# A decode kernel with grouped-query attention: the side's single-engine loads as three 64 KB rows in two source pieces, its multiplication later, its slot kept longer

## The chip, the cores and the metric

The kernel runs on one core of a Trainium2 chip. The metric is the device time in microseconds (us) of one execution. A core has five engines with their own instruction streams (TensorE for matrix products, VectorE, ScalarE, GpSimd and SyncE) and sixteen DMA engines, which carry all transfers from the chip's large memory (HBM) into the on-chip memory of 128 partitions. SyncE issues most transfers here, GpSimd a few.

## The reference

Two layers, each a decode step of attention with a cache and a gated feed-forward block, with the same weights and the same cache in both layers. Two sequences (b), one token each, 32 query heads on 8 key heads, 32768 cached positions of 128 numbers, all in 32 bits:

```python
for _ in range(2):
    h = layernorm(x)                                   # x: (2, 1, 512)
    q = (h @ wq).reshape(2, 1, 32, 128).transpose(0, 2, 1, 3)
    k, v = repeat(k_cache, 4, axis=1), repeat(v_cache, 4, axis=1)
    p = softmax(einsum("bhqd,bhkd->bhqk", q, k) * 128 ** -0.5)
    x = x + merge_heads(einsum("bhqk,bhkd->bhqd", p, v)) @ wo
    h = layernorm(x)
    gate, up = h @ W_gate, h @ W_up
    x = x + (relu(gate) * up) @ W_down
```

The keys and the values are 16 pairs (head, sequence) of 16 MB each; a layer reads all of them.

## The kernel before

**Turns and halves.** One pair of key head and sequence is a turn; a layer has 16. A turn's keys come in two halves of 8 MB (128 rows of 64 KB), its values too. A half has four pages of eight blocks of 512 columns. The on-chip memory has three slots of one half each, and behind them a small ring for everything else. The list `by_use` holds the slots in order of use: a load takes the first, and `used(s)` moves it to the end. A load into a slot waits, on SyncE, until the work that read the slot before is done; the loads behind it in SyncE's stream wait too.

**Order.** The loop `for i in range(1, NG)` takes the keys of turn i (`keys`, lines 427 to 460) and then the values of turn i - 1 (`values`, lines 462 to 495). `keys` is a generator that issues a half's load and then goes through its pages j = 0 to 7: `k_tile` multiplies a page, and at certain pages other work is put in between: the rest of the softmax of the turn before (`soft_tail`), the output of the turn before that (`head_out`), and in every second turn its projection (`project`, with a load of 1 MB of `wo`). All engines go through their instructions in the order in which this code issues them.

**The side.** In turn 11 of each layer (`SIDE_TURN`), the last 6 blocks of page 3 of the values (1.5 MB, a tenth of the turn's values) are not loaded as a part of their half but in another layout, which the host has prepared, and with another share for each DMA engine. `load_side` (line 315) takes a slot for it and issues four loads. One goes on SyncE's queue (line 318): 20 partitions, 48 KB each, in three pieces of 16 KB, a source of 5 rows, so that five DMA engines carry it. Three are single-engine loads on GpSimd's queue (line 322), each 4 partitions from row 28, 64 or 92 on, 48 KB each in three pieces of 16 KB: source and destination have no common factor in their outer sizes (3 and 4), so that one DMA engine carries all of it. Between them `turn_by` (line 307) issues a tiny transfer of single numbers over 7 or 6 DMA engines, which moves GpSimd's choice of the engine for the next load on by as many. The kernel is built with 512 bytes of room for GpSimd's descriptors (`SCRATCH`, line 32).

`side_keys` (line 281), called from `soft_tail` of turn 11, puts the probabilities into the side's layout: transposes on VectorE of windows of p into two tiles t and u, zeros from GpSimd, and two products with masks. `v_side` (line 325) multiplies them, 24 chunks of 512 columns on 96 partitions, into the accumulator of turn 11. It is issued in `keys(13)` at page 1 (line 450), followed by the evacuation of the accumulator on VectorE. At page 2 come `head_out` of turn 11 and the projection, with the load of `wo`.

**Slots around the side.** With a, b for the two other slots and s for the side's, `by_use` is [a, b, s] after `load_side`. The first half of turn 13's keys takes a, the second b; the first half of turn 12's values takes s, the second a.

Of the kernel before, what the change touches and what calls it, by code (L numbers as in the profile page):

```python
# [8 lines left out]
F32 = mybir.dt.float32  # L9
# [5 lines left out]
D = 512  # L15
# [27 lines left out]
SIDE_TURN = NG - 5  # L43
SIDE_PAGE, SIDE = 3, 6
SIDE_WAYS, SIDE_ROWS, SIDE_CHUNKS, SIDE_GAP = 5, 20, 24, 64
SIDE_END, ALONE, TURNED = 96, (28, 64, 92), (7, 0, 6)
SIDE_THIRD = SIDE_CHUNKS * D // 3 + 16

C_SAME, C_MEAN, C_SEL, C_PAIR, C_SIDE, C_ONE, C_MHALF, C_END = 0, 128, 160, 192, 224, 226, 227, 229

# [2 lines left out]
def attention_reglu_decode(ctx: ExitStack, tc: tile.TileContext, x, k, v, wq, wo, wgu, wd, consts, side, alone, out):  # L53
# [12 lines left out]
    def ring(at, width):  # L66
        if at < 0:
            assert at * KB + width <= 0 or (spill[0] + 1) * SLOT == RING
            at += (spill[0] + 1) * SLOT - RING
        at = int((RING + at) * KB)  # L70
        return arena[:, at : at + width]

    def slot(s, at=0, width=SLOT * KB):
        at = int((s * SLOT + at) * KB)
        return arena[:, at : at + width]
# [57 lines left out]
    col = sel[:, :NB]  # L133
    pair = cst[:, C_PAIR : C_PAIR + 32]
    side_rows = cst[:, C_SIDE : C_SIDE + 2]
    turned = sb.tile([4 * max(TURNED), NLAYER * len(TURNED)], F32, name="turned")
    mhalf = cst[:, C_MHALF : C_MHALF + NB]
    oT = sb.tile([P, REP, NB], F32, name="oT")
    qz = sb.tile([P, 2, QZ], F32, name="qz")
# [139 lines left out]


    def side_keys(p):
        W = SIDE_CHUNKS * 32
        t, u = (ring(SIDE_KEYS_AT + e * W / KB, W) for e in range(2))
        at = SIDE_PAGE // 2 % 2 * D + (SIDE_PAGE % 2 * 8 + 8 - SIDE) * 32

        def windows(c, start, step, n):
            rows = p[32 * c : 32 * c + 32]
            return bass.AP(rows.tensor, rows.offset + at + start, [rows.ap[0], [step, n], [1, 32]])

        def chunks(t, c, lo, n):  # L290
            return t[32 * c : 32 * c + 32, 32 * lo : 32 * (lo + n)].rearrange("p (k r) -> p k r", r=32)

        for g, c in enumerate((0, 1, 3)):
            nc.vector.transpose(chunks(t, 0, 8 * g, 8), windows(c, 0, 20, 8))
            nc.vector.transpose(chunks(u, 0, 8 * g, 8), windows(c, 132, 4, 8))
        nc.vector.transpose(chunks(t, 2, 0, 24), windows(2, 0, 4, 24))
        nc.vector.transpose(chunks(u, 2, 0, 24), windows(2, 68, 4, 24))
        for c in (1, 3):
            nc.gpsimd.memset(t[32 * c : 32 * c + 32], 0.0)
            nc.gpsimd.memset(u[32 * c : 32 * c + 32], 0.0)  # L300
        nc.vector.tensor_scalar_mul(t, t, side_rows[:, 0:1])
        nc.vector.scalar_tensor_tensor(t, u, side_rows[:, 1:2], t, ALU.mult, ALU.add)
        return t

    def turn_by(n):
        if n:
            few = consts[: 5 * n, :1].rearrange("(e r) f -> e r f", r=5)[:, :4]
            nc.gpsimd.dma_start(turned[: 4 * n, steps[0] : steps[0] + 1], few)  # L310
        steps[0] += 1

    steps, side_at = [0], {}

    def load_side(L, n):
        s = by_use[0]
        vt = side_at[n] = slot(s, 0, 3 * SIDE_THIRD).rearrange("p (a f) -> p a f", a=3)[:, :, : SIDE_CHUNKS * D // 3]
        load(vt[:SIDE_ROWS], side[L, :, : 4 * SIDE_CHUNKS * D])
        part = 4 * SIDE_CHUNKS * D // 3
        for e, (row, step) in enumerate(zip(ALONE, TURNED)):  # L320
            turn_by(step)
            nc.gpsimd.dma_start(vt[row : row + 4], alone[L, e, :, :part])
        used(s)

    def v_side(n):
        vt, t, J = side_at.pop(n), side_of.pop(n), SIDE_PAGE // 4
        for k in range(SIDE_CHUNKS):
            nc.tensor.matmul(  # L328
                acc[32 * (k % 4) : 32 * (k % 4) + 16, :],
                t[:SIDE_END, 32 * k + 16 * J : 32 * k + 16 * J + 16],  # L330
                vt[:SIDE_END, k // 8, k % 8 * D : (k % 8 + 1) * D],
                start=False, stop=k >= SIDE_CHUNKS - 4,
            )

    def v_tile(n, j, vt, first, last, blocks):
# [87 lines left out]
    for L in range(NLAYER):  # L423
        last = L == NLAYER - 1
        seq = list(range(NG)) if L % 2 == 0 else list(range(NG - 1, -1, -1))

        def keys(i):
            n = seq[i]
            if i < NG - 1:
                place_queries(i + 1, seq[i + 1])  # L430
            if L and i == 0:
                loads = list(kept_k)
                kept_k.clear()
            elif L and i == 1:
                f, g = key_slots
                loads = cuts(k, n, [(f, 0, 0, 8), (f, 16, 8, 16), (f, 32, 16, 32), (g, 0, 32, 48), (g, 32, 48, 64)])
            elif i == NG - 1:
                f, g = key_slots[:] = by_use[:2]
                loads = cuts(k, n, [(f, 0, 0, 32), (g, 0, 32, 48), (g, 32, 48, 64)])
            else:  # L440
                loads = whole(k, n)
            if not last and i == NG - 1:
                loads = list(loads)
                kept_k.extend(loads)
            for lo, _, t in by_page(loads):
                j = lo // 8
                k_tile(L, i, n, j, t)
                if L and i == 0:
                    yield
                if j == 1 and i == SIDE_TURN + 2:  # L450
                    v_side(seq[SIDE_TURN])
                    evacuate(seq[SIDE_TURN], False)
                if j == 1 and i >= 1:
                    soft_tail(L, i - 1, seq[i - 1])
                if j == 2 and i >= 2:
                    head_out(L, seq[i - 2])
                    if i % 2 == 1:
                        project((i - 3) // 2, load(ring(WO_AT, REP * D), wo[seq[i - 2] // NB]), False)
                    if i == NG - 1:
                        gather()  # L460

        def values(i, soft):
            n = seq[i]
            if i == NG - 1:
                if last:
                    s, t = by_use[:2]
                    pieces = [(s, 0, 0, 32), (t, 0, 32, 48), (t, 32, 48, 56)]
                else:
                    s = t = page_slot[0]
                    pieces = [(s, at, 8 * j, 8 * j + 8) for j, at in enumerate((0, 16, 32, 48, 0, 16, 32))]  # L470
                spill[0] = t
                pieces = chain(cuts(v, n, pieces), ending(n))
            elif i == NG - 2 and not last:
                page_slot[0] = by_use[0]
                pieces = cuts(v, n, [(by_use[0], 16 * (j % HALF), 8 * j, 8 * j + 8) for j in range(NT)])
            elif L and i == 0:
                f, g = key_slots
                pieces = chain(kept_v, aside, cuts(v, n, [(f, 0, 0, 16), (f, 32, 16, 22), (f, 48, 29, 32), (g, 0, 56, 64)]))
            else:
                pieces = whole(v, n, SIDE if i == SIDE_TURN else 0)  # L480
            first = True
            for lo, hi, t in by_page(pieces):
                v_tile(n, lo // 8, t, first, hi == BLOCKS and i != SIDE_TURN, range(lo % 8, lo % 8 + hi - lo))
                if not last and i == NG - 1 and lo in KEPT:
                    kept_v.append((lo, KEPT[lo], t[:, : (KEPT[lo] - lo) * D]))
                if not last and i == NG - 1 and hi == ASIDE[1]:
                    w = (ASIDE[0] - lo) * D
                    nc.vector.tensor_copy(sc_even.rearrange("p a b -> p (a b)"), t[:, w : w + 2 * D])
                if first and soft is not None:
                    soft_max(L, soft)  # L490
                first = False
            if i == SIDE_TURN:
                load_side(L, n)
            else:
                evacuate(n, i == NG - 1)

        first_keys = keys(0)
        queries(L, total, seq[0], first_keys if L else iter(()))
        list(first_keys)
        soft_max(L, seq[0])  # L500
        aside = []
        if L:
            nc.vector.memset(sums, 0.0)
            t = ring(ASIDE_AT, 2 * D)
            nc.vector.tensor_copy(t, sc_even.rearrange("p a b -> p (a b)"))
            aside.append((*ASIDE, t))
        for i in range(1, NG):
            list(keys(i))
            values(i - 1, seq[i])
        soft_tail(L, NG - 1, seq[NG - 1])  # L510
        head_out(L, seq[NG - 2])
        values(NG - 1, None)
        head_out(L, seq[NG - 1])
        project(HKV - 1, load(ring(LAST_WO_AT, REP * D), wo[seq[NG - 1] // NB]), True)
        total = feed_forward(L, add(op), by_use[:2] if last else None)
# [63 lines left out]
```

## Time and profile before

| | |
|---|---|
| median of three runs | 2596.72 us (2596.31 to 2596.78) |
| the profiled execution's own time | 2594.8 us |
| its span, first to last instruction | 2593.0 us |
| moved by DMA | 1105.89 MB, mean 426 GB/s |
| busy: TensorE, VectorE, ScalarE, GpSimd | 1306.7, 162.6, 41.3, 18.5 us |
| loads of `alone`: count, KB each | 6, 192.0 |
| load of `side`: count, KB each | 2, 960.0 |

The profile is of one execution. PE is TensorE, PEld its loading of weights, DVE VectorE, ACT ScalarE, POOL GpSimd, SP SyncE; "SPq" marks the issue of a transfer on SyncE's queue. L328 is line 328 of the kernel. A matrix product in 32 bits counts twice in the trace, so the 24 chunks of the side are x48. An arrow gives output and input by the program's names; all slots and the ring have the name arena. Queue q1 is SyncE's, q0 GpSimd's. The GB/s row has forty equal slices of the span, 64.8 us each.

### The profile page before, as it was taken

Reading aid. Unit: us, or ns where it says so; the run is one execution under the profiler, and the core shown is the slowest. Engines: PE = TensorE matmul, PEld = TensorE weight load, DVE = VectorE, ACT = ScalarE, POOL = GpSimd, SP = SyncE. Lnnn points to the kernel's source line nnn. Section 1 sums busy time; section 2 is a strip of 40 time slices with the busy share of each in tenths; the row PEclk is TensorE's granted clock in tenths of the full one; section 3 lists DMA queues with packets and bytes.
Section 4 is the critical chain, followed back from the end, with each engine's and each line's share of the span. In section 5 each row is a group of like instructions: output and inputs, shape, how many; then the busy total and the mean of one; then the engine's idle time right before and its main releaser. Section 6 shows DMA issues by size and latency. Waiting matters only on the chain.

```text
span 2593.0 us, 20044 instructions
## 1 busy us (share of the span) xinstructions
PE 1306.7 (50%) x9504; PEld 346.3 (13%) x9504; DVE 162.6 (6%) x379; ACT 41.3 (2%) x69; POOL 18.5 (1%) x27
## 2 busy tenths in 40 slices
PE   2544544554455444554675544554454445454456
PEld 0111111111111111111131111111111111111112
DVE  0000000000000010000010000000000000100001
ACT  0000000000000000000000000000000000000000
POOL 1000000000000000000000000000000000000000
PEclk9777777777777777777787777777777777777778
DMA  9999999999999999899999999999999999989998
GB/s 422 435 436 425 437 429 435 433 428 435 435 433 433 424 439 427 363 423 429 425 420 434 435 434 430 431 434 426 440 430 432 436 433 428 433 357 436 428 440 373
DMA packets 30835, 1105.89 MB, mean 426 GB/s; under 512 B 4570, under 2 KB 4834, under 8 KB 8034
## 3 DMA queue, kind: packets, MB, share of 16 engines
q1 hardware_dynamic: 29218, 1103.31, 98.8%
q8 instruction: 74, 1.21, 0.2%
q0 software_dynamic: 1376, 1.19, 0.1%
q10 hardware_dynamic: 160, 0.12, 0.0%
q14 instruction: 7, 0.06, 0.0%
HBM read 1104.53 MB, written 0.07 MB: 426 GB/s over the span
## 4 chain that ended last, share of the span: by engine, by line
DMA 66%; PE 23%; another core or an unknown queue 8%; issue 2%; DVE 0%; SPq 0%; POOL 0%; ACTq 0%; POOLq 0%; DVEq 0%
DMA arena<-k 47%; DMA arena<-v 12%; PE sc_odd L244 8%; PE sums L342 6%; PE sc_even L244 6%; DMA arena<-wo 2%; DMA arena<-wd 1%; DMA cst<-consts 1%; DMA arena<-alone 1%; PE sums L328 1%; PE sc_odd L213 1%; DMA arena<-wgu 1%; PE po L362 1%; PE sums L244 1%
## 5 line engine op out<-in xcount | busy, mean ns | idle before, releaser
L342 PE MATMUL sums<-arena 128*16 128x512 f32 (+1 forms) x4112 | 582.9, 719 | 599.9 <-DMA arena<-v 599.9
L244 PE MATMUL sc_odd<-arena,qz 128*32 128x512 f32 x2048 | 296.4, 733 | 281.6 <-DMA arena<-k 281.6
L244 PE MATMUL sc_even<-arena,qz 128*32 128x512 f32 x1920 | 276.8, 729 | 285.4 <-DMA arena<-k 285.4
L342 PEld LDWEIGHTS sums<-arena 128*16 128x16 f32 x4112 | 119.4, 109 | 1015.5 <-issue 515.8
L244 PEld LDWEIGHTS sc_odd<-arena,qz 128*32 128x32 f32 x2048 | 71.2, 132 | 487.4 <-DMA arena<-k 308.0
L244 PEld LDWEIGHTS sc_even<-arena,qz 128*32 128x32 f32 x1920 | 64.2, 130 | 472.6 <-DMA arena<-k 311.9
L356 DVE TENSOR_SCALAR arena<-sums,stat 128x512 f32<-128x512 f32 (+1 forms) x38 | 24.8, 665 | 857.6 <-PE sums L342 726.8
L269 DVE STREAM_TRANSPOSE arena<-arena 128x512 f32<-128x512 f32 x64 | 41.5, 686 | 2.5 <-ACT arena L262 2.5
L253 DVE TENSOR_REDUCE stat<-sc_odd 128x1 f32<-128x1024 f32 x16 | 19.6, 1225 | 319.2 <-PE sc_odd L244 319.2
L253 DVE TENSOR_REDUCE stat<-sc_even 128x1 f32<-128x1024 f32 x15 | 18.4, 1225 | 299.8 <-PE sc_even L244 299.8
L262 ACT ACTIVATE arena<-sc_odd,stat 128x1024 f32<-128x1024 f32 x16 | 17.8, 1114 | 1205.5 <-DVE stat L259 1205.5
L362 PE MATMUL po<-cst,arena 128*128 128x4 f32 x256 | 34.0, 256 | 2.1 <-DVE arena L356 2.1
L362 PEld LDWEIGHTS po<-cst,arena 128*128 128x128 f32 x256 | 31.2, 191 | 26.3 <-issue 21.8
L262 ACT ACTIVATE arena<-sc_even,stat 128x1024 f32<-128x1024 f32 x15 | 16.7, 1114 | 1063.2 <-DVE stat L259 915.7
L328 PE MATMUL sums<-arena 96*16 96x512 f32 x96 | 15.2, 799 | 31.3 <-DMA arena<-alone 16.3
L275 DVE RECIPROCAL stat<-sm 128x1 f32<-128x1 f32 x32 | 5.2, 162 | 374.9 <-PE sm L273 374.9
L259 DVE TENSOR_REDUCE stat<-mp 128x1 f32<-128x32 f32 x32 | 6.1, 192 | 356.3 <-PE mp L257 356.3
L397 PE MATMUL sc_odd<-arena 128*32 128x224 f32 x256 | 22.1, 499 | 12.6 <-DMA arena<-wgu 12.2
L373 PE MATMUL sums<-arena,oT 128*2 128x512 f32 x112 | 15.4, 623 | 16.2 <-DMA arena<-wo 12.9
L213 PE MATMUL sc_odd<-arena 128*32 128x512 f32 x128 | 20.1, 700 | 5.7 <-DMA arena<-wq 3.1
L257 PEld LDWEIGHTS mp<-arena,cst 128*128 128x128 f32 x64 | 12.7, 248 | 51.6 <-issue 49.9
L165 PE MATMUL meana<-cst,stat 128*128 128x32 f32 x4 | 1.0, 341 | 35.4 <-DMA cst<-consts 35.0
(76 smaller groups left out, 190.8 us busy)
## 6 DMA issues: line engine op xcount, KB each, us to landing
arena<-v SPq DMA_DIRECT2D x17, 2048.0 KB, 17.6
arena<-k SPq DMA_DIRECT2D x7, 4096.0 KB, 36.1
arena<-wo SPq DMA_DIRECT2D x16, 1024.0 KB, 51.0
arena<-v SPq DMA_DIRECT2D x2, 6656.0 KB
arena<-v SPq DMA_DIRECT2D x2, 4096.0 KB, 38.2
arena<-wgu SPq DMA_DIRECT2D x8, 896.0 KB, 7.6
arena<-wgu SPq DMA_DIRECT2D x4, 1792.0 KB, 21.1
arena<-wq SPq DMA_DIRECT2D x6, 1024.0 KB, 8.2
```

The costliest lines, as they stand in the source:

```text
L213: nc.tensor.matmul(qp[32 * c : 32 * c + 32, B, :], xT[:, kt, :], t[:, e * D : (e + 1) * D], start=kt == 0, stop=kt == KT - 1)
L244: nc.tensor.matmul(sc_of[n][32 * c : 32 * c + 32, B, :], qz[:, i % 2, 28 - 4 * j : 60 - 4 * j], kt[:, ch * D : (ch + 1) * D], start=j == 0 ...
L253: nc.vector.tensor_reduce(m1, sc_of[n], AX.XY, ALU.max)
L257: nc.tensor.matmul(mp[:, :32], same, mt, start=True, stop=True)
L262: nc.scalar.activation(p, sc_of[n].rearrange("p a b -> p (a b)"), AF.Exp, bias=nm[:, 0:1], scale=1.0, accum_out=rs)
L269: nc.vector.transpose(pT[:, B * D : (B + 1) * D], p[:, B * D : (B + 1) * D])
L328: nc.tensor.matmul(acc[32 * (k % 4) : 32 * (k % 4) + 16, :], t[:SIDE_END, 32 * k + 16 * J : 32 * k + 16 * J + 16], vt[:SIDE_END, k // 8, k ...
L342: nc.tensor.matmul(acc[32 * c : 32 * c + 16, e * w : (e + 1) * w], pT[:, B, m, 16 * J : 16 * J + 16], vt[:, at * D + e * w : at * D + (e + ...
L356: nc.vector.tensor_scalar_mul(acs[:, at : at + w], acc[:, at : at + w], linv[:, 0:1])
L362: nc.tensor.matmul(po[:, :REP], acs[:, t * P : (t + 1) * P], selh[:, 4 * t : 4 * t + 4], start=t == 0, stop=t == 3)
L373: nc.tensor.matmul(op[32 * u : 32 * u + NB, :], oT[:, u, :], w[:, u * D : (u + 1) * D], start=pair_at == 0, stop=pair_at == HKV - 2)
L397: nc.tensor.matmul(gu[32 * j : 32 * j + 32, s, :], xT[:, at + e, :], t[:, f : f + HF], start=at + e == 0 and s == 0, stop=at + e == KT - 1 ...
```

## The change

- The single-engine loads have 3 partitions of 64 KB (32 chunks) instead of 4 of 48 KB (24 chunks), from row 29, 64 or 93 on. The destination row is whole; the source has two pieces of 3 rows of 32 KB, so outer sizes 2 and 3. Bytes per load are as before.
- The load on SyncE's queue has the same bytes in the same five shares; its destination rows of 48 KB are no longer cut in three.
- The cursor's tiny transfers have 2 numbers for each engine instead of 4, over 7 and 6 engines as before.
- `side_keys` makes t for 32 chunks, and u in two halves of 16 chunks in half the room; three zeroings on GpSimd instead of four, ten transposes instead of eight, three products instead of two.
- `v_side` has 32 chunks instead of 24. It is issued at page 3 of `keys(13)` instead of page 1, and `head_out`, `project` and the load of `wo` in that turn at page 5 instead of page 2, which is behind the load of the second key half. `soft_tail` of turn 12, at page 1, comes ahead of `v_side` instead of behind it.
- `v_side` calls `used(s)` a second time, so `by_use` is [b, a, s] when the second key half is loaded: it still takes b, but the first half of turn 12's values takes a and the second takes s.
- The host arranges the side's data and the masks for this.

```diff
-SIDE_END, ALONE, TURNED = 96, (28, 64, 92), (7, 0, 6)
-SIDE_THIRD = SIDE_CHUNKS * D // 3 + 16
+TWENTIES, THREES = ((0, 9), (1, 9), (3, 6)), ((0, 4), (1, 4), (3, 24))
+ALONE, ALONE_CHUNKS, TURNED = (29, 64, 93), 32, (7, 0, 6)
...
     def side_keys(p):
-        W = SIDE_CHUNKS * 32
-        t, u = (ring(SIDE_KEYS_AT + e * W / KB, W) for e in range(2))
+        W, H = ALONE_CHUNKS * 32, ALONE_CHUNKS // 2
+        t, u = ring(SIDE_KEYS_AT, W), ring(SIDE_KEYS_AT + W / KB, W // 2)
...
+        nc.gpsimd.memset(t[32:64], 0.0)
+        nc.gpsimd.memset(u[32:64], 0.0)
+        nc.gpsimd.memset(t[:32, 32 * SIDE_CHUNKS :], 0.0)
+        lo = 0
+        for c, n in TWENTIES:
+            turn_windows(t, 0, lo, c, 0, 20, n)
+            lo += n
+        turn_windows(t, 2, 0, 2, 0, 3, ALONE_CHUNKS)
+        nc.vector.tensor_scalar_mul(t[:96], t[:96], side_rows[:96, 0:1])
+        for half in range(2):
+            lo = 0
+            for (c, n), (_, twenties) in zip(THREES, TWENTIES):
+                a, b = max(lo, H * half), min(lo + n, H * half + H)
+                if a < b:
+                    turn_windows(u, 0, a - H * half, c, 20 * twenties - 29 + 3 * (a - lo), 3, b - a)
+                lo += n
+            turn_windows(u, 2, 0, 2, 3 * ALONE_CHUNKS - 29 + 3 * H * half, 3, H)
+            w = t[:96, 32 * H * half : 32 * H * (half + 1)]
+            nc.vector.scalar_tensor_tensor(w, u[:96], side_rows[:96, 1:2], w, ALU.mult, ALU.add)
         return t
...
-            few = consts[: 5 * n, :1].rearrange("(e r) f -> e r f", r=5)[:, :4]
-            nc.gpsimd.dma_start(turned[: 4 * n, steps[0] : steps[0] + 1], few)
+            few = consts[: 3 * n, :1].rearrange("(e r) f -> e r f", r=3)[:, :2]
+            nc.gpsimd.dma_start(turned[: 2 * n, steps[0] : steps[0] + 1], few)
...
-        vt = side_at[n] = slot(s, 0, 3 * SIDE_THIRD).rearrange("p (a f) -> p a f", a=3)[:, :, : SIDE_CHUNKS * D // 3]
-        load(vt[:SIDE_ROWS], side[L, :, : 4 * SIDE_CHUNKS * D])
-        part = 4 * SIDE_CHUNKS * D // 3
+        vt = slot(s)
+        side_at[n] = s, vt
+        load(vt[:SIDE_ROWS, : SIDE_CHUNKS * D], side[L, :, : 4 * SIDE_CHUNKS * D].rearrange("e (r f) -> e r f", r=4))
         for e, (row, step) in enumerate(zip(ALONE, TURNED)):
             turn_by(step)
-            nc.gpsimd.dma_start(vt[row : row + 4], alone[L, e, :, :part])
+            nc.gpsimd.dma_start(vt[row : row + 3], alone[L, e, :, :3, : ALONE_CHUNKS * D // 2])
         used(s)
...
     def v_side(n):
-        vt, t, J = side_at.pop(n), side_of.pop(n), SIDE_PAGE // 4
-        for k in range(SIDE_CHUNKS):
+        (s, vt), t, J = side_at.pop(n), side_of.pop(n), SIDE_PAGE // 4
+        used(s)
+        for k in range(ALONE_CHUNKS):
...
-                if j == 1 and i == SIDE_TURN + 2:
+                if j == 1 and i >= 1:
+                    soft_tail(L, i - 1, seq[i - 1])
+                late = i == SIDE_TURN + 2
+                if late and j == 3:
                     v_side(seq[SIDE_TURN])
                     evacuate(seq[SIDE_TURN], False)
-                if j == 1 and i >= 1:
-                    soft_tail(L, i - 1, seq[i - 1])
-                if j == 2 and i >= 2:
+                if j == (5 if late else 2) and i >= 2:
                     head_out(L, seq[i - 2])
...
-        alone = np.zeros((NLAYER, len(ALONE), 3, 4 * W // 3 + SIDE_GAP), np.float32)
+        alone = np.zeros((NLAYER, len(ALONE), 2, 4, W // 2 + SIDE_GAP), np.float32)
```

More of the change, by code (lines that the diff above doesn't have):

```diff
@@ L135, in attention_reglu_decode @@
     side_rows = cst[:, C_SIDE : C_SIDE + 2]
-    turned = sb.tile([4 * max(TURNED), NLAYER * len(TURNED)], F32, name="turned")
+    turned = sb.tile([2 * max(TURNED), NLAYER * len(TURNED)], F32, name="turned")
     mhalf = cst[:, C_MHALF : C_MHALF + NB]
@@ L281, in side_keys, with turn_windows @@
     def side_keys(p):
-        W = SIDE_CHUNKS * 32
-        t, u = (ring(SIDE_KEYS_AT + e * W / KB, W) for e in range(2))
+        W, H = ALONE_CHUNKS * 32, ALONE_CHUNKS // 2
+        t, u = ring(SIDE_KEYS_AT, W), ring(SIDE_KEYS_AT + W / KB, W // 2)
         at = SIDE_PAGE // 2 % 2 * D + (SIDE_PAGE % 2 * 8 + 8 - SIDE) * 32
-        def windows(c, start, step, n):
+        def turn_windows(t, group, lo, c, start, step, n):
             rows = p[32 * c : 32 * c + 32]
-            return bass.AP(rows.tensor, rows.offset + at + start, [rows.ap[0], [step, n], [1, 32]])
@@ L290, in chunks @@
[L290 to L300, printed above, removed]
@@ L301, in side_keys @@
-        nc.vector.tensor_scalar_mul(t, t, side_rows[:, 0:1])
-        nc.vector.scalar_tensor_tensor(t, u, side_rows[:, 1:2], t, ALU.mult, ALU.add)
+            src = bass.AP(rows.tensor, rows.offset + at + start, [rows.ap[0], [step, n], [1, 32]])
+            to = t[32 * group : 32 * group + 32, 32 * lo : 32 * (lo + n)].rearrange("p (k r) -> p k r", r=32)
+            nc.vector.transpose(to, src)
+        nc.gpsimd.memset(t[32:64], 0.0)
+        nc.gpsimd.memset(u[32:64], 0.0)
+        nc.gpsimd.memset(t[:32, 32 * SIDE_CHUNKS :], 0.0)
@@ L316, in load_side @@
         s = by_use[0]
-        vt = side_at[n] = slot(s, 0, 3 * SIDE_THIRD).rearrange("p (a f) -> p a f", a=3)[:, :, : SIDE_CHUNKS * D // 3]
-        load(vt[:SIDE_ROWS], side[L, :, : 4 * SIDE_CHUNKS * D])
-        part = 4 * SIDE_CHUNKS * D // 3
+        vt = slot(s)
+        side_at[n] = s, vt
+        load(vt[:SIDE_ROWS, : SIDE_CHUNKS * D], side[L, :, : 4 * SIDE_CHUNKS * D].rearrange("e (r f) -> e r f", r=4))
         for e, (row, step) in enumerate(zip(ALONE, TURNED)):
             turn_by(step)
-            nc.gpsimd.dma_start(vt[row : row + 4], alone[L, e, :, :part])
+            nc.gpsimd.dma_start(vt[row : row + 3], alone[L, e, :, :3, : ALONE_CHUNKS * D // 2])
         used(s)
     def v_side(n):
-        vt, t, J = side_at.pop(n), side_of.pop(n), SIDE_PAGE // 4
-        for k in range(SIDE_CHUNKS):
+        (s, vt), t, J = side_at.pop(n), side_of.pop(n), SIDE_PAGE // 4
+        used(s)
+        for k in range(ALONE_CHUNKS):
             nc.tensor.matmul(
                 acc[32 * (k % 4) : 32 * (k % 4) + 16, :],
-                t[:SIDE_END, 32 * k + 16 * J : 32 * k + 16 * J + 16],
-                vt[:SIDE_END, k // 8, k % 8 * D : (k % 8 + 1) * D],
-                start=False, stop=k >= SIDE_CHUNKS - 4,
+                t[:96, 32 * k + 16 * J : 32 * k + 16 * J + 16],
+                vt[:96, k * D : (k + 1) * D],
+                start=False, stop=k >= ALONE_CHUNKS - 4,
             )
@@ L530 @@
     cst[:, C_PAIR : C_PAIR + 32] = np.equal.outer(rows // 4, np.arange(32))
-    cst[:, C_SIDE] = (rows < SIDE_ROWS) | (rows // 4 == 16)
-    cst[:, C_SIDE + 1] = (rows // 4 == 7) | (rows // 4 == 23)
+    cst[:, C_SIDE] = (rows < SIDE_ROWS) | (rows >= 64) & (rows < 67)
+    cst[:, C_SIDE + 1] = (rows % 64 >= 29) & (rows % 64 < 32)
     cst[:, C_ONE] = 1.0 / D
@@ L541, in side_blocks @@
     def side_blocks(v):
-        W = SIDE_CHUNKS * D
-        side = np.zeros((NLAYER, SIDE_WAYS, 4 * W + SIDE_GAP), np.float32)
-        alone = np.zeros((NLAYER, len(ALONE), 3, 4 * W // 3 + SIDE_GAP), np.float32)
+        W = ALONE_CHUNKS * D
+        side = np.zeros((NLAYER, SIDE_WAYS, 4 * SIDE_CHUNKS * D + SIDE_GAP), np.float32)
+        alone = np.zeros((NLAYER, len(ALONE), 2, 4, W // 2 + SIDE_GAP), np.float32)
         for L in range(NLAYER):
@@ L549, in side_blocks @@
             keys = keys.reshape(4, 32 * SIDE, D)
-            low = keys[[0, 1, 3]]
-            side[L, :, : 4 * W] = low[:, :160].reshape(3, 8, SIDE_ROWS, D).transpose(2, 0, 1, 3).reshape(SIDE_WAYS, 4 * W)
-            fours = (low[:, 160:], keys[2, :96], keys[2, 96:])
-            for e, rows in enumerate(fours):
-                rows = rows.reshape(SIDE_CHUNKS, 4, D).transpose(1, 0, 2)
-                alone[L, e, :, : 4 * W // 3] = rows.reshape(3, 4 * W // 3)
+            low = np.concatenate([keys[c, : SIDE_ROWS * m] for c, m in TWENTIES])
+            rows = low.reshape(SIDE_CHUNKS, SIDE_ROWS, D).transpose(1, 0, 2)
+            side[L, :, : 4 * SIDE_CHUNKS * D] = rows.reshape(SIDE_WAYS, -1)
+            rest = np.concatenate([keys[c, SIDE_ROWS * m :] for c, m in TWENTIES])
+            for e, threes in enumerate((rest, keys[2, :96], keys[2, 96:])):
+                rows = threes.reshape(ALONE_CHUNKS, 3, D).transpose(1, 0, 2)
+                alone[L, e, :, :3, : W // 2] = rows.reshape(2, 3, W // 2)
         return side, alone
```

## The prediction

> **What bounds the kernel now.** I read the page first: the span, the slices of the DMA engines, the queues and the chain that ended last.
>
> ```profile
> span 2593.0 us, 20044 instructions
> DMA  9999999999999999899999999999999999989998
> GB/s 422 435 436 425 437 429 435 433 428 435 435 433 433 424 439 427 363 423 429 425 420 434 435 434 430 431 434 426 440 430 432 436 433 428 433 357 436 428 440 373
> q1 hardware_dynamic: 29218, 1103.31, 98.8%
> DMA 66%; PE 23%; another core or an unknown queue 8%; issue 2%; DVE 0%; SPq 0%; POOL 0%; ACTq 0%; POOLq 0%; DVEq 0%
> ```
>
> The sixteen DMA engines are busy 98.8% of the span with SyncE's queue alone, so only an idle stretch of theirs can be won. Two slices stick out, at 363 and 357 GB/s among neighbours of about 430, one in each layer. The table by stages (columns as the second row names them; the last two are the DMA share and GB/s) cuts them out:
>
> ```profile
> core 0: us, PE busy (x) PEld busy (x) DVE busy (x) ACT busy (x) POOL busy (x), PEclk, DMA share, GB/s
> 0.00:979.00 979.00, 473.76 (x3312) 120.41 (x3316) 59.38 (x132) 15.74 (x25) 9.16 (x13) 0.75 1.00 432
> 979.00:1040.00 61.00, 22.34 (x162) 4.99 (x154) 1.73 (x4) 1.21 (x2) 2.58 (x4) 0.75 1.01 432
> 1040.00:1060.00 20.00, 11.32 (x78) 3.57 (x82) 2.18 (x5) 0.00 (x0) 0.00 (x0) 0.65 0.43 174
> 1060.00:2300.00 1240.00, 643.66 (x4680) 170.90 (x4672) 79.39 (x185) 20.00 (x34) 6.73 (x10) 0.75 1.00 431
> 2300.00:2325.00 25.00, 11.73 (x90) 3.78 (x94) 2.18 (x5) 0.00 (x0) 0.00 (x0) 0.73 0.63 261
> 2325.00:2570.00 245.00, 132.34 (x988) 35.77 (x979) 15.04 (x37) 3.62 (x6) 0.00 (x0) 0.76 1.00 429
> 2570.00:2593.00 23.00, 11.54 (x210) 6.93 (x210) 2.67 (x11) 0.72 (x2) 0.00 (x0) 0.85 0.73 299
> ```
>
> Outside the tail, the engines stand still in two places: 20 x 0.57 = 11.4 us in the first layer, 25 x 0.37 = 9.2 us in the second. Together 20.6 us: that is all a better order can win there.
>
> Why they stand still, from the timeline around the first place: SyncE's queue, then TensorE, then GpSimd (start, length, instruction, count, and in brackets the idle time before it and what ended that).
>
> ```profile
> 993.88 0.35 SPq L78 DMA_DIRECT2D arena<-k  x1
> 994.28 0.42 SPq L78 DMA_DIRECT2D arena<-wo  x1
> 1014.62 0.33 SPq L78 DMA_DIRECT2D arena<-k  x1
> 1056.49 6.49 SPq L78 DMA_DIRECT2D arena<-v  x2
> ```
> ```profile
> 1005.60 8.96 PE L342 MATMUL sums<-arena 128*16 128x512 f32 x64 [11.78 <-DMA arena<-v]
> 1027.18 4.99 PE L244 MATMUL sc_odd<-arena,qz 128*32 128x512 f32 x32 [12.62 <-DMA arena<-k]
> 1048.43 8.01 PE L328 MATMUL sums<-arena 96*16 96x512 f32 x48 [16.26 <-DMA arena<-alone]
> 1060.69 8.77 PE L244 MATMUL sc_odd<-arena,qz 128*32 128x512 f32 x80
> 1079.41 3.61 PE L342 MATMUL sums<-arena 128*16 128x512 f32 x16 [9.95 <-DMA arena<-v]
> 1098.79 8.44 PE L342 MATMUL sums<-arena 128*16 128x512 f32 x64 [9.44 <-DMA arena<-v]
> ```
> ```profile
> 979.27 1.33 POOL L322 DMA_DIRECT2D arena<-alone  x2 [934.48 <-PE sc_even L244]
> 980.59 0.59 POOL L310 DMA_DIRECT2D turned<-consts  x1
> 1018.88 0.66 POOL L322 DMA_DIRECT2D arena<-alone  x1 [37.70 <-issue]
> ```
>
> The first half of turn 13's keys lands at 1027.18. After two of its four pages TensorE reaches the side (L328) and waits until 1048.43 for the third single-engine load. Behind that wait stands everything of TensorE, and behind TensorE SyncE: turn 12's values go into the side's own slot, so their load is issued at 1056.49, when the side has been multiplied. The second key half, issued at 1014.62, has long run dry. From then on halves land 19.4 us apart (1079.41, 1098.79): DMA-bound again, the loss never made good. The second layer does the same:
>
> ```profile
> 2292.46 5.52 PE L244 MATMUL sc_odd<-arena,qz 128*32 128x512 f32 x32 [12.22 <-DMA arena<-k]
> 2313.01 7.18 PE L328 MATMUL sums<-arena 96*16 96x512 f32 x48 [15.04 <-issue]
> 2320.26 6.49 SPq L78 DMA_DIRECT2D arena<-v  x2
> 2343.89 3.62 PE L342 MATMUL sums<-arena 128*16 128x512 f32 x16 [10.67 <-DMA arena<-v]
> ```
>
> **The single-engine loads.** The view of the tile alone gives their time from issue to landing; the DMA view of 984 to 998.4 us gives the queue of GpSimd (packets, MB, share):
>
> ```profile
> DMA to landing us min/median/max: 29.3/39.4/49.4
> ```
> ```profile
> q0 software_dynamic: 95, 0.08, 1.7%
> ```
>
> 0.08 MB is five 16 KB pieces (0.082) in 14.4 us, one per 2.9 us. A half of the keys is eight 64 KB rows per engine in 19.4 us, so 2.42 us a row; a 16 KB piece at that rate is 0.6. So one piece goes out, then one row of SyncE's queue: 3.03 us a turn, twelve turns 36 us, which is the 39.4 us with some 3 us of start and end. The other 90 packets are 15 x 6: each of the other fifteen engines gets one tiny packet of the same load per row (14.4 / 2.42 = 6). So the loads queue up behind each other on every engine, which is why the second takes 49.4 us.
>
> The third is issued at 1018.88, 0.2 us after the first landed (979.27 + 39.4 = 1018.67): GpSimd had no room for its descriptors until then. That is my reading of the 37.70 us marked "issue".
>
> Here the Trainium skill speaks differently: "DMA: Bandwidth & Descriptors", section "Queues, rings and completion order", says that an engine drains a whole packet, typically 9 to 17 descriptors, from one queue before it switches. By that rule twelve pieces would leave in one go and their number would be no matter; the rows above show one piece per switch, so the trace disagrees. The sum below would be the same by the rule, only the slower rival would fall away.
>
> **The change, part by part.**
>
> *Pieces.* Source pieces are 32 KB and the destination row is 64 KB whole; taking the shorter, as before (16 KB of 64), six pieces per load. One costs 1.2 us, a turn 3.63. The two loads and the step of the cursor ahead of the third need 6 + 6 + 2 = 14 turns of 2.42 us on its engine, 34 us, then its own six 21 us; with 5 us at the start and 1 at the end, 61 us after 979.3: it lands at about 1040. Two of its loads and the step now take about half the descriptors, so I expect the third to fit and be issued by 982. Bounds: if it still waits for the first (979.3 + 6 x 3.63 + 3 = 1004) and then takes between 29.3 and 49.4 us, 1034 to 1054. I take 1040, between them.
>
> *The side's slot and place.* Turn 12's first value half now goes into the slot of turn 13's first key half, and the side is multiplied after page 3, not page 1. So SyncE waits only for four pages from 1027.18: two pages are 4.99 us, so 10 us, issue at about 1037. The queue then still holds the second key half. The second value half takes the side's slot and is issued when the side is done: 32 chunks are 8.01 x 32/24 = 10.7 us, from 1040 to 1051. The first value half keeps the engines busy until 1027.18 + 2.4 (wo, 1 MB) + 2 x 19.4 = 1068. Margin 17 us; the load's issue has to stand by about 1065, so the third single-engine load may land as late as 1054 at no cost. What is late next is nothing in this turn: page 7 of turn 13 ends by about 1063, and its slot is wanted after the second value half, at 1087. Nothing is left of the idle time, and by landings the gain is 1079.41 - 1068.4 = 11.0 us here and 2343.89 - (2292.46 + 2.4 + 38.8) = 10.2 in the second layer, 21.2 against the 20.6 of the idle shares.
>
> *What is queued behind the new wait.* TensorE at page 3: the four pages of the second half, which land no earlier than 1046 anyway. VectorE: the evacuation, as before.
>
> *The head's output, wo and the projection, moved from page 2 to page 5.* Twelve or so short products and one copy on VectorE change places within TensorE's work on this half. The load of wo passes the second key half on SyncE's queue, 2.4 us of transfer that only swaps its turn. It lands at 1049 or so, before page 5 at about 1057. No cost; if it were late, TensorE has the margin of 17 us.
>
> *VectorE.*
>
> ```profile
> 943.60 0.97 DVE L296 STREAM_TRANSPOSE arena<-arena 32x768 f32<-32x768 f32 x1
> 945.46 0.62 DVE L301 TENSOR_SCALAR arena<-arena,cst 128x768 f32<-128x768 f32 x1
> 946.18 1.02 DVE L302 SCALAR_TENSOR_TENSOR arena<-arena,cst 128x768 f32<-128x768 f32 x1
> 956.83 0.17 DVE L275 RECIPROCAL stat<-sm 128x1 f32<-128x1 f32 x1 [9.63 <-PE sm L273]
> ```
>
> Transposes go from 3072 columns in eight to 3840 in ten (by 0.97 per 768, 1.0 us more); the products from 1.64 us over 768 columns to 2.2 over 1024, one of them in two. Some 2 us more, all inside the 9.63 us in which VectorE waits for TensorE next: nothing. Uncovered, it would be 2 us in each layer, 4 in all. GpSimd's zeroing happens ahead of all this: nothing.
>
> *The side's load on SyncE.* 16 KB pieces become 48 KB rows, the same 960 KB over the same five engines: at 2.42 us per 64 KB no difference I can price; between minus and plus 1 us.
>
> Sum: 20.6 us by shares, 21.2 by landings; I take 20, a little under both, since the shares are rounded and an idle moment may remain. The profiled execution took 2594.8 us (span 2593.0), so 2574.8; the median of the runs shown is 2596.72, 1.9 more, so **2576.7**. Below 0.2%, 5.2 us, a measurement of this kernel can't be told from no change.
>
> **Rivals.**
>
> *The second value half becomes the late one* (8%). If the third load lands not at 1040 but at about 1060, the side ends at 1071 and the load misses its 1065 by 6 us in each layer: 2576.7 + 12 = 2589. For it: the load stays behind two others. Against: the upper bound above is 1054.
>
> *The rows go to other engines than meant* (4%): if the cursor's steps, now of two elements per engine, moved it otherwise, two of the loads would share an engine, 192 KB or 7.2 us more on it per layer, and the halves wait for their last engine: 2576.7 + 14.4 = 2591. Against: both steps keep their 7 and 6 rows of source.
>
> *No change* (4%): the engines win the gap but the end is set by one that had no gap. The engine of the third load had pieces until 1048, so its own gap was some 9 us; so at most 2595, and little speaks for it.
>
> *Slower* (4%): the pieces stay at 16 KB, because the destination is cut otherwise than I think. Then the third load is still issued at 1019, and it has lost its help: wo's short rows no longer come ahead of the second key half, so 24 foreign turns at 2.42 from 984 reach to 1042, its own twelve at 3.03 to 1079, landing 1081. The side ends at 1092 against an empty queue from 1068: 25 us idle instead of 11.4 and 9.2, together about 29 us: 2626. It decides from a landing at about 1068, where the old gap is back. Against: the pieces now are the shorter of source and destination.
>
> **How the numbers follow.** The forecast has 80%, its own range 2574 (gain 22.7, the landings' 21.2 and the side's 1 us) to 2580 (a fifth of the gain lost). To leave out no more than 2 in 10, with its tails, the range goes to 2587, into the first rival. Faster by over 0.2%: 80 + 8 + 2 of the second rival = 0.90. Within 0.2%: 4 + 2 = 0.06. Slower: 0.04.
>
> **What would show it.** Right: the DMA share at 1.00 through the place now at 0.43; both slices near 430 GB/s; SyncE's first value load some 10 us after turn 13's first keys, not 29; GpSimd's third load issued within 3 us of the first two; landings of about 27, 41 and 59 us; the side starting at its fourth page or a few us later. Wrong: a gap between the two value loads with an idle DMA, TensorE waiting for alone past 1065, or a 37 us "issue" on GpSimd that is still there.

## The result: 2572.76 us, 0.9908 of before

The changed kernel's median is 2572.76 us (2572.19 to 2572.99, four runs), that of the kernel before, measured with it, 2596.51 (2595.93 to 2596.78). The ratio is 0.9908, its 95% interval 0.9891 to 0.9926: faster by 23.75 us, where 20 were forecast. The time lies 1.2 us below the predicted range. The profiled execution took 2572.99 us, against 2594.8 before: 21.8 us less.

The page of the changed kernel, span, slices and SyncE's queue:

```profile
span 2571.1 us, 20109 instructions
GB/s 425 427 436 437 428 435 433 435 428 437 427 436 435 427 437 431 430 433 426 422 413 433 436 431 433 434 431 435 429 437 432 432 434 431 433 431 432 428 435 383
q1 hardware_dynamic: 29138, 1103.31, 99.6%
```

The slices of 363 and 357 GB/s are gone. The table by stages (the last two columns are DMA share and GB/s) shows the two places at full share, and the end as the only stage that isn't:

```profile
1040.00:1060.00 20.00, 17.05 (x136) 5.26 (x140) 0.92 (x2) 0.00 (x0) 0.00 (x0) 0.83 0.99 427
2300.00:2325.00 25.00, 18.93 (x148) 5.35 (x144) 2.38 (x4) 0.00 (x0) 0.00 (x0) 0.84 1.03 442
2550.00:2571.00 21.00, 11.53 (x210) 6.92 (x210) 2.67 (x11) 0.71 (x2) 0.00 (x0) 0.84 0.75 310
```

The timeline around the first place, SyncE's queue, TensorE and GpSimd (L245 are keys, L354 values, L340 the side), then the time of the first layer's three single-engine loads from issue to landing:

```profile
1015.34 0.43 SPq L79 DMA_DIRECT2D arena<-wo  x1
1036.15 16.19 SPq L79 DMA_DIRECT2D arena<-v  x2
```
```profile
1027.08 5.12 PE L245 MATMUL sc_odd<-arena,qz 128*32 128x512 f32 x32 [12.20 <-DMA arena<-k]
1032.44 3.64 PE L245 MATMUL sc_odd<-arena,qz 128*32 128x512 f32 x32
1042.69 9.26 PE L340 MATMUL sums<-arena 96*16 96x512 f32 x64 [6.61 <-DMA arena<-alone]
1068.26 3.28 PE L354 MATMUL sums<-arena 128*16 128x512 f32 x16 [7.15 <-DMA arena<-v]
...
2322.61 3.61 PE L354 MATMUL sums<-arena 128*16 128x512 f32 x16 [5.82 <-DMA arena<-v]
```
```profile
980.25 1.24 POOL L331 DMA_DIRECT2D arena<-alone  x2 [936.46 <-PE sc_even L245]
981.48 0.58 POOL L319 DMA_DIRECT2D turned<-consts  x1
982.06 0.61 POOL L331 DMA_DIRECT2D arena<-alone  x1
```
```profile
DMA to landing us min/median/max: 26.0/42.2/60.4
```

GpSimd issues the third load 0.6 us after the step of the cursor, and it lands at 982.06 + 60.4 = 1042.5. The first value half is issued at 1036.15, when page 3 is done, and lands at 1068.26 instead of 1079.41: 11.15 us won. In the second layer it lands at 2322.61 instead of 2343.89, 21.28 us for both layers.

### The profile page after: what moved, and what is told of

The parts are those of the page before. It is cut to its first block, busy times and chain, and to the rows that moved or that the text cites. A ratio compares the mean times of both kernels' runs of the same rounds, so it can differ in the third digit from the quotient of the medians.

```text
span 2571.1 us, 20109 instructions
## 1 busy us (share of the span) xinstructions
PE 1319.3 (51%) x9536; PEld 345.7 (13%) x9536; DVE 166.6 (6%) x385; ACT 41.3 (2%) x69; POOL 15.9 (1%) x25
## 3 DMA queue, kind: packets, MB, share of 16 engines
q1 hardware_dynamic: 29138, 1103.31, 99.6%
## 4 chain that ended last, share of the span: by engine, by line
DMA 69%; PE 23%; another core or an unknown queue 7%; DVE 0%; issue 0%; ACTq 0%; SPq 0%; POOL 0%; POOLq 0%; DVEq 0%
DMA arena<-k 47%; DMA arena<-v 19%; PE sc_odd L245 9%; PE sums L354 7%; PE sc_even L245 5%; DMA arena<-wd 1%; DMA cst<-consts 1%; DMA arena<-wgu 1%; PE sc_odd L214 1%; PE sums L245 1%; PE sums L385 1%; PE po L374 1%; DMA arena<-wq 0%; PE mp L258 0%
## 5 line engine op out<-in xcount | busy, mean ns | idle before, releaser
L354 PE MATMUL sums<-arena 128*16 128x512 f32 (+1 forms) x4112 | 583.9, 721 | 589.1 <-DMA arena<-v 589.0
L245 PE MATMUL sc_odd<-arena,qz 128*32 128x512 f32 x2048 | 299.3, 738 | 278.8 <-DMA arena<-k 278.8
L245 PE MATMUL sc_even<-arena,qz 128*32 128x512 f32 x1920 | 280.1, 737 | 283.7 <-DMA arena<-k 283.7
L354 PEld LDWEIGHTS sums<-arena 128*16 128x16 f32 x4112 | 119.2, 109 | 1003.2 <-issue 513.4
L245 PEld LDWEIGHTS sc_odd<-arena,qz 128*32 128x32 f32 x2048 | 71.4, 132 | 486.3 <-DMA arena<-k 304.7
L245 PEld LDWEIGHTS sc_even<-arena,qz 128*32 128x32 f32 x1920 | 65.0, 132 | 473.4 <-DMA arena<-k 310.3
L254 DVE TENSOR_REDUCE stat<-sc_odd 128x1 f32<-128x1024 f32 x16 | 19.6, 1225 | 305.8 <-PE sc_odd L245 305.8
L340 PE MATMUL sums<-arena 96*16 96x512 f32 x128 | 18.9, 759 | 13.3 <-issue 6.7
L258 PEld LDWEIGHTS mp<-arena,cst 128*128 128x128 f32 x64 | 13.5, 263 | 53.5 <-issue 51.8
```

The lines of the kernel that those rows point to most:

```text
L245: nc.tensor.matmul(sc_of[n][32 * c : 32 * c + 32, B, :], qz[:, i % 2, 28 - 4 * j : 60 - 4 * j], kt[:, ch * D : (ch + 1) * D], start=j == 0 ...
L254: nc.vector.tensor_reduce(m1, sc_of[n], AX.XY, ALU.max)
L258: nc.tensor.matmul(mp[:, :32], same, mt, start=True, stop=True)
L340: nc.tensor.matmul(acc[32 * (k % 4) : 32 * (k % 4) + 16, :], t[:96, 32 * k + 16 * J : 32 * k + 16 * J + 16], vt[:96, k * D : (k + 1) * D], ...
L354: nc.tensor.matmul(acc[32 * c : 32 * c + 16, e * w : (e + 1) * w], pT[:, B, m, 16 * J : 16 * J + 16], vt[:, at * D + e * w : at * D + (e + ...
```

## The experiments

Theory: the third single-engine load is late because each piece on GpSimd's queue waits for a row of SyncE's queue, on every engine; the number of pieces is what the change makes smaller, and the time won is DMA engines that no longer stand still. Rivals: GpSimd's room for descriptors makes it late; or the place and the slot of the side, not the loads, bring the gain. A second question came with the miss: why the median moved by 2 us more than the profiled time.

**The kernel before, as a control.** No edit.

> The kernel before, unchanged: a control. The forecast of 2576.7 put the profiled time of before (2594.8) and its median (2596.72) 1.9 us apart and kept that distance for the changed kernel, which showed none (2572.99 profiled, 2572.76 median). Theory A: 2594.8 was one low execution; here the profiled time lies within 0.5 us of the median, both near 2596.5. Theory B: executions with a profile of the kernel before are about 1.8 us shorter than those without, whatever the execution; here again 2594.5 to 2595.0 beside a median near 2596.5. In both the idle time of the DMA engines at the side is 20 to 23 us over the two layers.

Measured: 2597.85 us (2595.38 to 2599.47, ten runs), ratio 0.9997 (0.9988 to 1.0007); the profiled execution took 2598.92. Theory B is out: here the profiled execution is 1.1 us longer than the median. Theory A's own figures missed too (within 0.5 us, near 2596.5), but what it says stands: the distance of 1.9 us belonged to one low execution. Its 2594.8 us is below all 48 other runs of the kernel before, of which the lowest took 2595.18. Twenty of them, on the control's chip, lie between 2595.44 and 2601.01, while the four of the changed kernel lie within 0.8 us. SyncE's queue in the control, and the table at the second layer's start and at its side, first in the execution that the prediction used, then in the control:

```profile
q1 hardware_dynamic: 29218, 1103.31, 98.7%
```
```profile
1320.00:1380.00 60.00, 44.38 (x400) 17.71 (x404) 9.61 (x28) 1.21 (x2) 0.72 (x1) 0.84 1.02 429
2300.00:2330.00 30.00, 16.73 (x134) 5.23 (x138) 2.18 (x5) 0.00 (x0) 0.00 (x0) 0.77 0.69 289
```
```profile
1320.00:1380.00 60.00, 44.38 (x388) 14.15 (x392) 10.61 (x32) 1.21 (x2) 0.72 (x1) 0.81 0.99 415
2300.00:2330.00 30.00, 15.22 (x114) 4.46 (x110) 2.17 (x5) 0.00 (x0) 0.00 (x0) 0.71 0.63 262
```

The span is 2597.1 us, so the queue's packets took 98.7% of it, 2563 us; in the execution before the change 98.8% of 2593.0, 2562; in the changed kernel 99.6% of 2571.1, 2561. That is one amount within the rounding (0.05% is 1.3 us). What differs is idle time: of the 4.1 us by which the control's span is longer, 60 x 0.03 = 1.8 us are at the second layer's start and 30 x 0.06 = 1.8 at the second side.

**The place and the slot alone.** The kernel before with

```diff
     def load_side(L, n):
...
+        at_slot[n] = s
...
     def v_side(n):
...
+        used(at_slot.pop(n))
...
-                if j == 1 and i == SIDE_TURN + 2:
+                if j == 1 and i >= 1:
+                    soft_tail(L, i - 1, seq[i - 1])
+                late = i == SIDE_TURN + 2
+                if late and j == 3:
                     v_side(seq[SIDE_TURN])
...
-                if j == 2 and i >= 2:
+                if j == (5 if late else 2) and i >= 2:
```

> The place and the slot alone: loads of 4 rows of 48 KB in 16 KB pieces as before, but the side at page 3, the head's output, projection and wo at page 5, and the first value half in the other slot. Theory (turns): the third load has 28 turns of others ahead of it on its engine at 2.42 us, from 984 us to about 1052, five pieces of its own at 3.03 until SyncE's queue is empty at 1068 and the rest without turns, landing near 1072; the side ends at 1080, the second value half comes some 13 us late in each layer, total 2595 to 2605: no gain from the place alone. Rival (room): the third load lands some 29 us after its issue at 1019, as in the kernel before, so at 1048; then nothing is late and the time is that of the changed kernel, 2573.

Measured: 2588.41 us (2586.66 to 2589.8), 0.9965 (0.9952 to 0.9978). Theory and rival both missed. TensorE at the side, the table around the gap, and GpSimd's queue from 1038.5 to 1044.8 us:

```profile
1062.99 7.75 PE L330 MATMUL sums<-arena 96*16 96x512 f32 x48 [26.75 <-DMA arena<-alone]
```
```profile
1060.00:1080.00 20.00, 16.76 (x132) 5.14 (x136) 0.96 (x3) 0.00 (x0) 0.00 (x0) 0.80 0.69 286
2320.00:2340.00 20.00, 12.81 (x100) 4.00 (x104) 0.92 (x2) 0.00 (x0) 0.00 (x0) 0.73 0.74 304
```
```profile
q0 software_dynamic: 101, 0.15, 6.4%
```

The third load lands at 1063: 15 us later than in the kernel before, and still 9 earlier than I had worked out. The working left out wo. Its 128 rows of 8 KB pass in SyncE's queue just then (the trace has them between 1038 and 1048 us, 0.31 to 0.35 us each), and a turn beside such a row is short: nine pieces of 16 KB (0.15 MB, of two loads) went out in 6.3 us, where the kernel before had five in 14.4. Whether 28 turns of others were ahead or fewer, the trace doesn't tell: a packet's record has no engine. The gap is 6.2 and 5.2 us instead of 11.4 and 9.2. So the place and the slot win 9 us with the old loads, though the load itself comes later by them.

**The loads alone.** The changed kernel without the second `used(s)`, with the side at page 1 ahead of soft_tail and the head's output, wo and projection at page 2.

> The loads alone: 3 rows of 64 KB in 32 KB pieces, the side's keys for 32 chunks, but the side at page 1, the head's output and wo at page 2, and the first value half in the side's slot. Theory (turns): six pieces per load bring the third load in at 1032 to 1036 (wo's short rows shorten some turns), the side runs 1036 to 1046, the value load is issued at 1046 when the second key half is about to end (1044 to 1049 by engine): 0 to 3 us idle per layer, total 2573 to 2579, so most of the gain comes from the loads. Rival (the place decides): the side still ends too late, near 1053, some 7 us idle per layer, total 2586 to 2590.

Measured: 2572.91 us (2572.12 to 2573.16), 0.9904 (0.9889 to 0.9919): the changed kernel's time, and the theory's lower end of 2573. SyncE's queue, TensorE, and the first layer's landings; then GpSimd's queue while the third load's six pieces pass, here (1018 to 1027.2 us) and in the changed kernel (1018 to 1037.6):

```profile
995.10 0.42 SPq L79 DMA_DIRECT2D arena<-wo  x1
1016.06 0.33 SPq L79 DMA_DIRECT2D arena<-k  x1
1039.95 6.48 SPq L79 DMA_DIRECT2D arena<-v  x2
```
```profile
1026.92 6.08 PE L245 MATMUL sc_odd<-arena,qz 128*32 128x512 f32 x32 [10.94 <-DMA arena<-k]
1032.84 7.04 PE L339 MATMUL sums<-arena 96*16 96x512 f32 x64
1068.12 3.61 PE L353 MATMUL sums<-arena 128*16 128x512 f32 x16 [10.59 <-DMA arena<-v]
```
```profile
DMA to landing us min/median/max: 26.8/40.8/46.7
```
```profile
q0 software_dynamic: 109, 0.20, 5.6%
q0 software_dynamic: 115, 0.20, 2.6%
```

With wo ahead of the second key half again, its short rows come earlier: the same six pieces (0.20 MB) need 9.2 us instead of 19.6, and the third load lands at 981.24 + 46.7 = 1028, 14.5 us earlier than in the changed kernel and 4 to 8 earlier than expected. The side follows page 1 without a wait, and the value load is issued at 1039.95, before the second key half is through. The new loads bring all of the gain alone.

**Twelve pieces.** The changed kernel with

```diff
-            nc.gpsimd.dma_start(vt[row : row + 3], alone[L, e, :, :3, : ALONE_CHUNKS * D // 2])
+            nc.gpsimd.dma_start(vt[row : row + 3], alone[L, e, :, :3, : ALONE_CHUNKS * D // 4])
```

and a source of four pieces on the host.

> The changed kernel with the sources of the single-engine loads in four pieces of 16 KB instead of two of 32 KB: the same 3 rows, the same bytes, place and slots, twelve pieces per load again. Theory (turns): the third load is again issued only when the first has landed (about 1019), 26 turns of others reach to 1047, its own twelve end near 1071, the side at 1081, some 13 us idle per layer: 2595 to 2603, the whole gain gone. Rival (the piece count is no matter, only rows, place and slot are): 2572 to 2575.

Measured: 2593.3 us (2590.91 to 2597.01), 0.9984 (0.9974 to 0.9993). GpSimd, and TensorE at the side:

```profile
980.78 0.64 POOL L319 DMA_DIRECT2D turned<-consts  x1
1018.60 0.64 POOL L331 DMA_DIRECT2D arena<-alone  x1 [37.18 <-issue]
```
```profile
1063.13 10.29 PE L340 MATMUL sums<-arena 96*16 96x512 f32 x64 [26.25 <-DMA arena<-alone]
```

Same rows, bytes, place and slots, and 20.5 us of the gain are gone: the piece count decides. The third load lands at 1063, as in the run with the place alone, and beside the same short rows of wo, not at 1071; the time is 1.7 us below the theory's range. Against the run with the place alone it is 4.9 us slower, and TensorE's side takes 10.29 us instead of 7.75: where the side is late, its eight more chunks cost 2.5 us in each layer.

**More room for descriptors.** The kernel before with

```diff
-SCRATCH = 512
+SCRATCH = 1024
```

and two tiles of the ring moved to make the space.

> The kernel before with 1024 bytes of room for GpSimd's descriptors instead of 512 (some room in the ring is used twice for it); loads, pieces, place and slots as before. Theory (turns): the third load is issued with the others, near 981, and its 37 us of idle time ahead of the issue are gone, but it still waits on its engine behind the 24 turns of the two others and lands near 1048: total 2595 to 2600, no gain. Rival (room): the late issue is what makes it late; it lands by 1030 and the total is 2573 to 2580.

Measured: 2600.33 us (2597.36 to 2601.04), 1.0009 (1.0 to 1.0018), 0.3 above the theory's range and far from the rival's. GpSimd, landings, TensorE:

```profile
980.14 0.58 POOL L310 DMA_DIRECT2D turned<-consts  x1
980.72 0.66 POOL L322 DMA_DIRECT2D arena<-alone  x1
```
```profile
DMA to landing us min/median/max: 39.7/49.1/67.5
```
```profile
1048.48 7.44 PE L328 MATMUL sums<-arena 96*16 96x512 f32 x48 [15.04 <-DMA arena<-alone]
```

The 37.70 us of waiting at the issue are gone and nothing is won: issued at 980.72 instead of 1018.88, the third load lands 67.5 us later at the same 1048. The reading of the "issue" as a lack of room was right; as a cause of the lateness it is excluded.

**The old slot.** The changed kernel without the second `used(s)`.

> The changed kernel without the second used: new loads, side at page 3, but the first value half goes into the side's slot again. Theory: with the third load in at 1042 the side ends near 1052, so the first value half is issued at 1052 instead of 1036, while the engines run dry between 1044 and 1049 (wo included, 1051): 2 to 6 us idle per layer, total 2577 to 2584. So the slot is needed where the side stands late, and only there. Rival (with the new loads the slot is no matter either way): 2572 to 2574.

Measured: 2584.21 us (2583.47 to 2586.29), 0.9953 (0.9938 to 0.9968), 0.2 above the theory's upper end. SyncE's queue, TensorE and the table:

```profile
1049.65 0.80 SPq L79 DMA_DIRECT2D arena<-v  x2
```
```profile
1040.84 8.76 PE L339 MATMUL sums<-arena 96*16 96x512 f32 x64 [4.24 <-DMA arena<-alone]
```
```profile
1040.00:1060.00 20.00, 17.65 (x144) 5.60 (x144) 2.10 (x3) 0.00 (x0) 0.00 (x0) 0.91 0.78 319
2295.00:2320.00 25.00, 18.72 (x152) 5.39 (x144) 2.35 (x4) 0.00 (x0) 0.00 (x0) 0.86 0.78 322
```

The value load waits for the side again and comes 13.5 us later; 4.4 and 5.5 us of idle time, 11.4 us in the total. So at page 3 the slot is needed; with the side at page 1 it isn't.

**Once more the kernel before.**

> The kernel before, unchanged, for one more look at where its executions differ. Theory: the span minus the idle time of the DMA engines is the same 2570 us in every execution, and the idle time is what varies; here too idle time at the sides is 20 to 23 us, and the time 2595 to 2600. Rival: the work itself (rate of the engines) varies.

Measured: one execution, 2596.94 us, span 2595.2. The table at the second layer's start and at the second side:

```profile
1320.00:1380.00 60.00, 45.88 (x392) 17.95 (x396) 10.53 (x32) 1.21 (x2) 0.71 (x1) 0.80 1.02 427
2300.00:2330.00 30.00, 16.00 (x122) 5.02 (x126) 2.18 (x5) 0.00 (x0) 0.00 (x0) 0.72 0.63 265
```

SyncE's queue has 98.7% of the span, 2561 us: the same amount again within the rounding. The second side has a share of 0.63, as in the control, and the second layer's start 1.02, as in the execution that the prediction used. The work stays, the idle time varies.

**No side at all.** The changed kernel without `load_side`, `side_keys` and `v_side`; turn 11's values come as two whole halves and its accumulator is evacuated with them; the head's output, wo and projection are at page 2 in every turn. The slots start in the order 1, 2, 0.

> The changed kernel without a side: the six blocks are loaded with their half, all of it over sixteen engines, no single-engine loads, no side's keys and no side's product (the slots start in another order, so that the ring's parts meet). The output is the same sum. Theory: the side only shifts bytes between engines, and the trace shows every engine at 2.42 us a row and busy, so the worth of the shift is at most half of 192 KB at that rate, 3.6 us per layer: 2572 to 2580. Rival: the shift is worth more than that, or its cost is larger than its worth: outside of that range.

Measured: 2577.84 us (2577.08 to 2578.98), 0.9926 (0.9909 to 0.9943), inside the theory's range. Its table, and the first of the two stages in the changed kernel:

```profile
1200.00:1260.00 60.00, 38.13 (x268) 9.08 (x268) 4.42 (x9) 1.21 (x2) 0.00 (x0) 0.78 0.97 410
2550.00:2576.00 26.00, 16.42 (x244) 9.25 (x244) 3.68 (x15) 0.71 (x2) 0.00 (x0) 0.73 0.73 304
```
```profile
1200.00:1260.00 60.00, 39.09 (x268) 9.08 (x268) 4.42 (x9) 1.21 (x2) 0.00 (x0) 0.77 0.99 420
```

Without the side there is more idle time: 60 x 0.03 = 1.8 us near the first layer's end against 60 x 0.01 = 0.6, and 26 x 0.27 = 7.0 at the end against 21 x 0.25 = 5.3. That is 2.9 of the 5.8 us by which the span is longer (2576.9 against 2571.1). It would fit engines that end more unevenly, but no view here shows them one by one. The side is worth 5.1 us where it is in time; in the kernel before it was late and cost 20 us net.

## Why the prediction was right or wrong

**What bounds, and where the gain is: right.** The work of SyncE's queue stayed at 2561 to 2563 us, and of the idle time nearly all was won at the two places: 20.6 us by shares, beside 0.9 at the end (23 x 0.27 = 6.2 before, 21 x 0.25 = 5.3 now).

**Pieces and turns: right, with most of their sizes.** Six pieces per load show in the packets of GpSimd's queue, before and now:

```profile
q0 software_dynamic: 1376, 1.19, 0.1%
q0 software_dynamic: 800, 1.18, 0.1%
```

The 576 packets fewer are 6 loads x 6 pieces x 16 engines. The third load landed at 1042.5 (forecast 1040, bounds 1034 to 1054), the landings were 26.0, 42.2 and 60.4 us (27, 41 and 59). The trace's records of this queue bear out the turns: its first packet is at 984.0, the second load's pieces begin at 998.8 and the third's at 1018.2, which is 6.1 and 14.1 turns of 2.42 us later, as with 6 and with 6 + 6 + 2. The third's own pieces took 19.4 us (forecast 21), and its landing came 5.0 us after the last of them (forecast 1), behind five packets without data. That the sum came so close is partly luck.

The runs with twelve pieces and with more room show that the turns make the load late, not the issue. In the working of the slower rival the landing at 1081 was wrong: wo's short rows don't stop helping when they move, they pass some 19 us later, and the load lands at 1063. The run with twelve pieces has that rival's condition, and it took 2593.3, not 2626: not slower at all.

**The side's slot and place: right for what happens, incomplete as to what it is for.** The value load was issued at 1036.15 (1037), the value half landed at 1068.26 (1068.4), the side ran 9.3 us (10.7). But the prediction moved loads, place and slot at once and never asked what the loads bring without the others. They bring everything. Moving wo behind the second key half makes the third load some 14 us later, and the later place and the other slot make up for just that.

**wo, projection, VectorE, GpSimd, SyncE's side load at no cost: right in the sum.** wo's transfer did more than swap its turn, as just said, but inside the margin. SyncE's load of the side is not shown apart; the work of its queue stayed the same within the rounding. In the changed kernel VectorE waits 7.41 us for TensorE behind the longer side's keys, 9.63 before:

```profile
956.90 0.17 DVE L276 RECIPROCAL stat<-sm 128x1 f32<-128x1 f32 x1 [7.41 <-PE sm L274]
```

2.2 us more work, 2 forecast.

**The sum: the step that failed.** "The profiled execution took 2594.8 us (span 2593.0), so 2574.8; the median of the runs shown is 2596.72, 1.9 more, so 2576.7." The 1.9 us were carried over to the changed kernel as if they were a constant beside the gain. The control shows that they are idle time of the kernel before which varies from execution to execution (2595.4 to 2601 on one chip), and that the profiled one was low. The changed kernel's executions lie within 0.8 us, and its median, 2572.76, is 0.2 below its profiled time instead of 1.9 above it. That is 2.1 us of the 3.9 by which the forecast was off. The other 1.8: the two ways to work out the gain gave 20.6 and 21.2, I took 20, "a little under both", and the profiled times differ by 21.8. By landings 21.3 of these are at the two places. The range's low end of 2574 allowed a gain of 22.7 us, though the two parts that it names, 21.2 and 1, make 22.2. Counted from the profiled 2594.8, 22.7 would have reached down to 2572.1; it was counted from the median.

**Open.** Why the idle time of the kernel before varies: in the control it sat at the second side and at the second layer's start, in the last execution of the kernel before at the second side alone; nothing here takes that apart. That it goes with the gap at the side is likely, not shown. From the fastest to the slowest run, the kernels that keep a gap differ by 2.8 us (old slot, four runs), 3.1 (place alone, five), 3.7 (more room, ten) and 6.1 (twelve pieces, ten), those without one by 0.8 (the changed kernel), 1.0 (loads alone) and 1.9 (no side), four runs each.

## What to carry to other kernels

Where one resource is busy nearly all the time, forecast the changed time from its work and the idle time that must remain, not as the old median less a gain: the old median may hold idle time that goes with what the change removes. When a change has several parts, price each one with the others left out. A load that shares DMA engines with a stream of large rows is priced by its number of pieces, one row of the stream for each.

## What the runs showed of the hardware

- A single-engine load on GpSimd's queue takes turns on all sixteen engines: sixteen packets for each of its pieces (576 fewer for 36 pieces fewer), of which one carries the data. Loads on different engines therefore wait for each other: in the changed kernel's first layer they land 26.0, 42.2 and 60.4 us after issue, in the order of issue.
- What stands in SyncE's queue sets the length of those turns: beside 1 MB in short rows (8 KB) the third load's six pieces took 9.2 us, beside rows of 64 KB 19.6.
- The room for GpSimd's descriptors set when the third load was issued, not when it landed: with 512 bytes it was issued at 1018.88, with 1024 at 980.72, and it landed at 1048 both times.
